# Fetching the last unit's other pair early, and splitting the last transfers over two queues, in an attention and MLP block

## The chip, the cores and the metric

The kernel runs on one core of a Trainium2 chip. The metric is the time of one execution in device microseconds (us), less being better. The core has a matrix engine (TensorE, "PE" in the profile, its weight loads "PEld"), a vector engine (VectorE, "DVE"), an activation engine (ScalarE, "ACT"), GpSimd ("POOL"), and SyncE ("SP"), which here does nothing but issue transfers. A row with "ACTq" or "SPq" is a transfer being issued from ACT or from SP.

## The reference

One input of 2048 tokens by 640 features is normalised. One branch is self-attention with 32 heads of 20 features, the other a two-layer MLP with 1536 hidden features and a normalisation of its own; the output is input plus both branches, in float32.

```python
def _A_ref(x, wqkv, wo):
    qkv = (x @ wqkv).reshape(B, S, 3, H, Dh).transpose(2, 0, 3, 1, 4)
    q, k, v = qkv[0], qkv[1], qkv[2]
    scores = jnp.einsum("bhqd,bhkd->bhqk", q, k) * (Dh ** -0.5)
    p = _softmax(scores, axis=-1)
    o = jnp.einsum("bhqk,bhkd->bhqd", p, v)
    return o.transpose(0, 2, 1, 3).reshape(B, S, D) @ wo

def _B_ref(x, w1, b1, w2, b2):
    y = _layernorm(x, axis=-1)
    h = _gelu(jnp.einsum("bsd,df->bsf", y, w1) + b1)
    return jnp.einsum("bsf,fd->bsd", h, w2) + b2

xn = _layernorm(x, axis=-1)
return x + _A_ref(xn, A_wqkv, A_wo) + _B_ref(xn, B_w1, B_b1, B_w2, B_b2)
```

## The kernel before

**Attention.** The heads are taken in 16 pairs, and the 2048 queries in two halves of 1024 (`hf` 0 and 1). For a pair and a half, `scores` (L680, exponential on ACT in L682) makes blocks of 128 keys by 512 queries for both heads, and `pv` (L711) multiplies them with the values. Values carry a column of ones, so the product `o` holds the unnormalised results and the softmax sums together. It has two parts `p` for either head, which are to be added. After 512 queries ACT reads `o` out into `ev` (L732); after 1024, `unload` writes the sums to the DRAM tensor `lpart` and the results to `opart`.

**Units and finishing.** Pairs are finished in units of three or two (`UNITS`). `finish` loads a unit's two parts of the sums into `lt` and of the results into `oa`, adds the parts of the sums, takes the reciprocal (L810 to L817), spreads it over the rows, adds the parts of the results (L835), multiplies (L837), splits the product into two float16 halves (L839, L841) and stores them in `oscr` (L842). `ready[hf]` counts the finished units of a half.

**The last unit** is pairs 14 and 15 of half 1. Its last pair never goes through DRAM: its rows of `lt` and `oa` are copied from `ev` itself (L778, L805), those of pair 14 come from `lpart` and `opart` (L774, L802). All these transfers are issued from ACT, because `dma` chooses ACT's queue for the last pair. For this unit the reciprocals are spread by sixteen products on PE with a selection matrix `sel` into a PSUM tile `rb` (L826), one of the three buffers of the pool `psS`.

**Projection.** `projection` multiplies `oscr` with the output weights in eight chunks of 256 tokens. A chunk has four groups of 15 products `z` (L1024). After each group DVE adds the result to the rows of `acc` (L983), and after two groups SP issues the store of the output (L987). Chunks 0 to 3 need half 0 alone, chunks 4 to 7 need the last unit too. `load_piece` has SP issue two transfers for `ot` (L977) and one for `acc` (L978). Behind the loop over the blocks (`ended`), the groups of `z` take their PSUM tiles from `psS`, the pool that `rb` is taken from.

**Order.** Every engine's order is written by hand. The loop calls `tick` after every two blocks of scores; `tick` advances all generators in `sides` by one step, so a `yield` in `finish` is a wait of one tick in the order, not a wait on the chip. Behind the loop one tick goes with three `z` products. `W1` is the number of ticks between the last unit's loads and the use of its sums, `W2` that between the spread reciprocals and the sum of the results.

**Completion semaphores.** The transfers issued from SP and ACT use eight completion semaphores in turn, counted in program order over both queues. A transfer therefore waits, on the engine that issues it, until the transfer eight places earlier has landed.

Of the kernel before, what the change touches and what calls it, by code (L numbers as in the profile page):

```python
# [7 lines left out]
F32 = mybir.dt.float32  # L8
# [8 lines left out]
P = 128  # L17
S, D, H, DH, F = 2048, 640, 32, 20, 1536
# [7 lines left out]
NPAIR = H // 2  # L26
# [7 lines left out]
UNITS = (3, 3, 3, 3, 2, 2)  # L34
# [8 lines left out]
def mha_mlp_kernel(tc, x, wqkv, wo, w1, b1, w2, b2, out):  # L43
    nc = tc.nc
# [3 lines left out]
    with (  # L48
# [13 lines left out]
        opart = dram.tile([2, D, S], F32, name="opart")  # L62
        lpart = dram.tile([2, 2, H, S // 2], F32, name="lpart")
# [529 lines left out]
        with ExitStack() as scope:  # L593
            pool = lambda **kw: scope.enter_context(tc.tile_pool(reuse_waits="tile", **kw))
            m0 = pool(name="m0", bufs=2)
            m1 = pool(name="m1", bufs=1)
            ptp = pool(name="pt", bufs=2 * GRP - 1)
# [3 lines left out]
            sides, patient = [], []  # L601
# [134 lines left out]
            def dma(g, hf):  # L736

                return (nc.scalar if (g, hf) == ORDER[-1] else nc.sync).dma_start
# [17 lines left out]
            fins, direct = [], []  # L756
            ready = [0, 0]

            def finishing():
                while fins:  # L760
                    yield from fins[0]
                    fins.pop(0)

            def finish(g0, g1, hf):
                nh, r0, r1 = 2 * (g1 - g0), 2 * g0 * DH, 2 * g1 * DH
                last = (g1 - 1, hf) == ORDER[-1]
                go = dma(g1 - 1, hf)
                w = 1024 if last else 512
                lt = m1.tile([P, 2, 64], F32, tag="lt", name="lt")
                n = checks.pop()  # L770
                yield
                gd = g1 - 1 if last else g1
                for p in range(2):
                    go(lt[: (gd - g0) * 32, p, :], lpart[p, hf, 2 * g0 : 2 * gd, :].rearrange("h (b t) -> (h b) t", t=64))  # L774
                    for a in range(2 if last else 0):

                        r = 64 * a + PAD + DH + VW * p
                        go(lt[(nh - 2 + a) * 16 : (nh - 1 + a) * 16, p, :],  # L778
                           direct[0][r : r + 1].rearrange("o c (b t) -> o (c b) t", t=64))
                for c0 in range(0, 1024, w):  # L780
                    cols = slice(hf * 1024 + c0, hf * 1024 + c0 + w)
                    if last:
                        o0, o1 = (ptp.tile([P, 2, 512], F32, tag="p", name="oa").rearrange("p c t -> p (c t)")
                                  for _ in range(2))
                        rb = o0

                        sel = [ptp.tile([P, 2, 512], F32, tag="p", name="sel").rearrange("p c t -> p (c t)")
                               for _ in range(2)]
                        for b0, t in zip((0, 8), sel):
                            nc.gpsimd.tensor_copy(  # L790
                                t[: nh * 16, : 8 * nh * DH].rearrange("p (b h d) -> p b h d", b=8, h=nh),
                                ident[: nh * 16, : nh * 16].rearrange("p (h b) -> p b h", b=16)[:, b0 : b0 + 8, :, None]
                                .to_broadcast([nh * 16, 8, nh, DH]))
                    else:
                        o = m1.tile([P, 2, 512], F32, tag="oa", name="oa")
                        o0, o1 = o[:, 0], o[:, 1]
                        rb = m1.tile([P, 512], F32, tag="rb", name="rb")
                    hl = o1.bitcast(F16).rearrange("p (s t) -> p s t", s=2)[: r1 - r0]
                    o0, o1, rb = o0[: r1 - r0], o1[: r1 - r0], rb[: r1 - r0]
                    rd = 2 * gd * DH - r0  # L800
                    for p, o in enumerate((o0, o1)):
                        go(o[:rd], opart[p, r0 : r0 + rd, cols])  # L802
                        for a in range(2 if last else 0):
                            q0 = 64 * a + PAD + VW * p
                            go(o[rd + a * DH : rd + (a + 1) * DH], direct[0][q0 : q0 + DH].rearrange("d c t -> d (c t)"))  # L805
                    if c0 == 0:
                        for _ in range(W1 if last else 4):
                            yield
                        l = lt[: nh * 16]
                        nc.vector.tensor_add(l[:, 0], l[:, 0], l[:, 1])  # L810

                        nc.vector.tensor_scalar(l[:, 1], l[:, 0], LO, None, ALU.is_ge, ALU.min,
                                                accum_out=good[: nh * 16, n : n + 1])
                        if not last:
                            yield
                        nc.vector.tensor_scalar(l[:, 0], l[:, 0], 1e-30, None, ALU.max)
                        nc.vector.reciprocal(l[:, 1], l[:, 0])  # L817
                        if not last:
                            go(linv[hf, 2 * g0 : 2 * g1, :].rearrange("h (b t) -> (h b) t", t=64), l[:, 1])
                        for _ in range(4 if last else 1):  # L820
                            yield
                    if last:

                        rb = psS.tile([P, 2, 512], F32, tag="s", name="rb")[: nh * DH]
                        for b in range(16):
                            nc.tensor.matmul(rb[:, b // 8, b % 8 * 64 : b % 8 * 64 + 64],  # L826
                                             sel[b // 8][: nh * 16, b % 8 * nh * DH : (b % 8 + 1) * nh * DH],
                                             l[:, 1], start=True, stop=True)
                        rb = rb.rearrange("p c t -> p (c t)")
                    for h in range(0 if last else nh):  # L830
                        go(rb[h * DH : (h + 1) * DH],
                           linv[hf, 2 * g0 + h : 2 * g0 + h + 1, c0 : c0 + w].to_broadcast([DH, w]))
                    for _ in range(W2 if last else 4):
                        yield
                    nc.vector.tensor_add(o0, o0, o1)  # L835
                    yield
                    nc.vector.tensor_mul(o0, o0, rb)  # L837
                    yield
                    nc.vector.tensor_copy(hl[:, 0], o0)  # L839
                    yield  # L840
                    nc.vector.tensor_sub(hl[:, 1], o0, hl[:, 0])  # L841
                    go(oscr[:, r0:r1, cols].rearrange("s d t -> d s t"), hl)  # L842
                ready[hf] += 1
# [111 lines left out]
            def mlp():  # L955
                load_chunk(0)
                load_chunk(1)
                yield 0.0
                for mc in range(NMC + 1):
                    first = [layer1(mc, f) for f in range(0, KF, 2)] if mc < NMC else []  # L960
                    second = [layer2(mc - 1, j, hf) for j in range(MC // P) for hf in range(2)] if mc else []
                    done[0] = mc == NMC
                    for i in range(6):
                        for part in first[i : i + 1] + (second[i - 1 : i] if i else []):
                            yield from part
# [29 lines left out]

            done = [False]
            ended = [False]
            W1, W2 = 12, 9

            def projection():  # L1000
                known = lambda c: split_done and ready[2 * c // NMC] == len(UNITS)
# [48 lines left out]
            def chain():  # L1050
                yield from mlp()
                yield from projection()


            with tc.manual_schedule():
                fill = chain()
                credit = 0.0 - next(fill)
                rate = 1.235
                groups = [(g, hf, cc, kb) for g, hf in ORDER for cc in range(2) for kb in range(0, NKB, GRP)]
# [40 lines left out]
                        sides.append(load_stack(*n, *([stacks[g, hf][1]] if n[0] == g else [])))  # L1100
                n = 0
                ended[0] = True

                def more(k):
                    nonlocal n
                    for _ in range(k):
                        n += 1
                        cost = next(fill, 0)
                        if n % 1 == 0 or cost is None:
                            tick()  # L1110
                        if cost == 0:
                            return False
                    return True
# [107 lines left out]
```

## Time and profile before

| | |
|---|---|
| three runs | 1362.19, 1363.1 and 1364.39 us; median 1363.1 us |
| the profiled execution | 1364.71 us |
| its span, first to last instruction | 1363.0 us |
| granted clock of TensorE over the span | 0.998 |
| PE busy | 1335.1 us, 98% |
| ACT busy | 1129.6 us, 83% |
| DVE busy | 1060.5 us, 78% |
| last read-out of `o` (L732) | 1290.43 us |
| last product starts its DVE step (L983) | 1356.27 us |

Times within the profile are counted from the start of the span. A row of the timeline gives start, length, engine, line, operation and tiles; rows of one kind that follow each other are merged, with their number. In brackets stands the idle time before it and what ended that. The length of an issue row (ACTq, SPq) is the time that the engine's queue takes to issue, not the transfer's time.

### The profile page before, as it was taken

How to read it: one execution, taken by the hardware profiler on the slowest of the kernel's cores; microseconds unless marked ns; L12 is line 12 of the kernel's file. 1: busy time of each engine (PE TensorE's matmuls, PEld its weight loads, DVE VectorE, ACT ScalarE, POOL GpSimd, SP SyncE). 2: the span in 40 equal slices, each digit the busy share in tenths (PEclk: the TensorE clock that was granted, in tenths of full speed). 3: DMA queues.
4: the chain of work that ended last, by engine and by line, in shares of the span. 5: the costliest groups of instructions: out<-in, count | busy, mean ns of one | idle time of the engine just before them, and what ended most of it. 6: DMA issues, size and time to landing. Idle time of an engine off the chain costs nothing.

```text
span 1363.0 us, 29029 instructions
## 1 busy us (share of the span) xinstructions
PE 1335.1 (98%) x11651; PEld 591.6 (43%) x11651; DVE 1060.5 (78%) x1436; ACT 1129.6 (83%) x1305; POOL 30.2 (2%) x74
## 2 busy tenths in 40 slices
PE   9999999999999999999999999999999999999998
PEld 6545545443334334433433343434433333333465
DVE  6658835998779897978797789897879898888732
ACT  6654525999999999999999999999999999999700
POOL 2000000000000000000000000000000000000000
PEclk9999999999999999999999999999999999999999
DMA  9868731111113221212321141223032223244275
GB/s 269 270 157 154 146 101 57 34 52 43 48 58 94 62 83 60 52 50 84 93 71 51 37 109 48 86 62 86 19 87 85 70 81 86 59 135 118 88 233 175
DMA packets 103073, 127.94 MB, mean 94 GB/s; under 512 B 27516, under 2 KB 69568, under 8 KB 102932
## 3 DMA queue, kind: packets, MB, share of 16 engines
q1 hardware_dynamic: 99864, 119.60, 31.2%
q0 software_dynamic: 2304, 5.24, 2.4%
q8 instruction: 93, 1.52, 0.5%
q10 hardware_dynamic: 764, 1.18, 0.3%
q14 instruction: 48, 0.39, 0.1%
HBM read 80.50 MB, written 42.51 MB: 90 GB/s over the span
## 4 chain that ended last, share of the span: by engine, by line
PE 79%; DVE 9%; ACT 7%; issue 3%; DMA 2%; ACTq 0%; SPq 0%; DVEq 0%
PE o L711 26%; PE s L680 17%; PE py L945 11%; PE pu L913 9%; PE qkp L322 8%; PE vp L395 5%; ACT p L682 4%; PE z L1024 4%; DVE low L694 3%; DMA oa<-ev 1%; DVE u L849 1%; DMA qkscr<-qkhl 1%; DVE u L850 1%; DVE w L853 1%; DVE w L854 1%
## 5 line engine op out<-in xcount | busy, mean ns | idle before, releaser
L682 ACT ACTIVATE p<-s 128x1024 f32<-128x1024 f32 x1024 | 972.3, 1041 | 43.4 <-PE s L680 37.0
L694 DVE TENSOR_TENSOR low<-p 128x1024 f16<-128x1024 f32 x512 | 610.7, 1219 | 159.9 <-ACT p L682 159.7
L711 PE MATMUL o<-p,vfull 128*32 128x512 bf16 (+1 forms) x4096 | 430.8, 493 | 0.0
L680 PE MATMUL s<-qs,ks 61*128 61x512 f16 x2048 | 316.5, 382 | 7.4 <-ACT p L682 6.5
L680 PEld LDWEIGHTS <-ks 61*128 61x128 f16 x2048 | 63.7, 94 | 293.6 <-issue 291.3
L913 PE MATMUL pu<-xm,w1t 128*128 128x256 f16 x1440 | 179.3, 274 | 1.4 <-DVE u L849 1.4
L945 PE MATMUL py<-w2t,hT 128*128 128x320 f16 x1152 | 178.5, 300 | 1.5 <-DVE u L849 1.5
L913 PEld LDWEIGHTS <-w1t 128*128 128x128 f16 x1440 | 130.5, 98 | 68.8 <-issue 55.1
L945 PEld LDWEIGHTS <-hT 128*128 128x128 f16 x1152 | 102.4, 98 | 88.6 <-issue 54.3
L322 PE MATMUL qkp<-xnt,wv 128*128 128x512 f16 x600 | 132.7, 383 | 2.3 <-DVE qkhl L338 2.1
L711 PEld LDWEIGHTS <-vfull 128*32 128x32 f16 x3072 | 60.8, 95 | 139.8 <-issue 108.5
L711 PE MATMUL o<-low,vfull 128*32 128x512 f16 x1024 | 104.0, 378 | 4.3 <-DVE low L694 4.3
L322 PEld LDWEIGHTS <-wv 128*128 128x128 f16 x600 | 58.7, 99 | 73.2 <-issue 2.6
L711 PEld LDWEIGHTS o<-p,vfull 128*32 128x32 f32 x2048 | 62.6, 108 | 51.3
L337 ACT ACTIVATE qkhl<-qkp,qks 128x1024 f16<-128x1024 f32 (+1 forms) x24 | 23.2, 968 | 66.5 <-PE qkp L322 43.3
L1024 PE MATMUL z<-w1t,ot 128*128 128x320 f16 x480 | 66.7, 300 | 1.8 <-DVE oa L837 1.8
L395 PE MATMUL vp<-wv,xnt 128*128 128x320 f16 x480 | 66.7, 299 | 0.0
L338 DVE SCALAR_TENSOR_TENSOR qkhl<-qkp,qks,qkhl 128x1024 f16<-128x1024 f32 (+1 forms) x24 | 26.5, 1105 | 45.3 <-ACT qkhl L337 44.5
L1024 PEld LDWEIGHTS <-ot 128*128 128x128 f16 x480 | 46.3, 98 | 23.1 <-issue 2.9
L395 PEld LDWEIGHTS <-xnt 128*128 128x128 f16 x480 | 46.7, 98 | 18.7
L983 DVE SCALAR_TENSOR_TENSOR acc<-z,sc,acc 128x320 f32<-128x320 f32 x32 | 17.5, 550 | 43.2 <-PE z L1024 39.9
L732 ACT ACTIVATE ev<-o 128x512 f32<-128x512 f32 x64 | 39.2, 612 | 4.2 <-PE o L711 4.1
(179 smaller groups left out, 666.7 us busy)
## 6 DMA issues: line engine op xcount, KB each, us to landing
qkscr<-qkhl SPq DMA_DIRECT2D x40, 256.0 KB
opart<-ev SPq DMA_DIRECT2D x124, 80.0 KB
ks<-qkscr SPq DMA_DIRECT2D x120, 80.0 KB
qs<-qkscr SPq DMA_DIRECT2D x192, 40.0 KB
oa<-opart SPq DMA_DIRECT2D x32, 240.0 KB
xt<-in_A_x_dram SPq DMA_DIRECT2D x16, 320.0 KB
xscr<-xnt SPq DMA_DIRECT2D x4, 1280.0 KB
xm<-xscr SPq DMA_DIRECT2D x8, 640.0 KB
```

Source lines behind the costliest of these rows:

```text
L322: nc.tensor.matmul(ps[:, i, :], wv[:, k, q, a, mm * P : (mm + 1) * P], xnts[c][:, k, b, :], start=(k + n == 0), stop=(k == KD - 1 and n == 2))
L337: nc.scalar.activation(hl[:, 0, i0:i1], ps[:, i0:i1], AF.Copy, scale=a)
L338: nc.vector.scalar_tensor_tensor(hl[:, 1, i0:i1], ps[:, i0:i1], a, hl[:, 0, i0:i1], ALU.mult, ALU.subtract)
L395: nc.tensor.matmul(ps[:, hf, :320], xnts[c][:, k, a, j * P : (j + 1) * P], wv[:, k, 2, b, hf * 320 : (hf + 1) * 320], start=(n == 0), stop ...
L680: nc.tensor.matmul(ps[:, a, :], ks[64 * a : 64 * a + 61, kb * P : (kb + 1) * P], qs[64 * a : 64 * a + 61, cc * 512 : (cc + 1) * 512], star ...
L682: nc.scalar.activation(pt, ps, AF.Exp, scale=QS)
L694: nc.vector.tensor_sub(low, pt, upper(pt))
L711: nc.tensor.matmul(pv.o[32 * q : 32 * q + 32, :], src[:, v0 - PAD * (1 - q % 2) :][:, :32], t, start=q not in pv.begun, stop=last, skip_gr ...
L732: nc.scalar.activation(evs[g, hf][:, cc], pv.o, AF.Copy)
L913: nc.tensor.matmul(ps[:, i], w1v[:, k, (f + i) // 4, a, fo_ : fo_ + P], xnt[:, k, b, :], start=(n == 0), stop=(n == 3 * KD - 1))
L945: nc.tensor.matmul(ps[:, :320], hTs[mc][:, f, a, j * P : (j + 1) * P], w2v[:, f, b, hf * 320 : (hf + 1) * 320], start=(n == 0), stop=(n == ...
L1024: nc.tensor.matmul(ps[:, :320], ot[:, k, a, j * P : (j + 1) * P], wov[:, k, b, h * 320 : (h + 1) * 320], start=(n == 0), stop=(n == 3 * KD ...
```

## The change

A generator `fetch_sums` runs with the other side work and, once five units of half 1 are finished, has SP issue the two loads of pair 14's sums into `lt`. A function `fetch_results` is called at the loop's end and has SP issue the two loads of pair 14's results into the two `oa` tiles. The last unit's `finish` takes these tiles and no longer issues those four loads. Its four copies of sums from `ev` stay on ACT's queue; its four copies of results from `ev` go to SP's queue. `W1` becomes 10 instead of 12, `W2` 5 instead of 9.

The order of instructions that results: PE's spread products `rb` stand six `z` products earlier (48 of them stand between the end of the last `pv` and `rb`, against 54). On DVE the four steps on the sums stand one L983 earlier, L835 and L837 one L983 earlier, and L839 and L841 two and one. On SP the two loads of sums stand ahead of a store to `accscr`, the two loads of results ahead of a store of the output, and the four copies of results between that store and the next. Nothing else is moved on PE, DVE or ACT. The two copies of `sel` on POOL take buffers that come free later, the first behind one and the second behind the next group of value products.

```diff
+            fetched = []
+
+            def fetch_sums():
+                while ready[1] < len(UNITS) - 1:
+                    yield
+                lt = m1.tile([P, 2, 64], F32, tag="lt", name="lt")
+                r = 2 * (NPAIR - UNITS[-1])
+                for p in range(2):
+                    nc.sync.dma_start(lt[: 32 * (UNITS[-1] - 1), p, :],
+                                      lpart[p, 1, r : 2 * NPAIR - 2, :].rearrange("h (b t) -> (h b) t", t=64))
+                fetched.append(lt)
+
+            def fetch_results():
+                r0, r1 = 2 * (NPAIR - UNITS[-1]) * DH, (2 * NPAIR - 2) * DH
+                for p in range(2):
+                    o = ptp.tile([P, 2, 512], F32, tag="p", name="oa").rearrange("p c t -> p (c t)")
+                    nc.sync.dma_start(o[: r1 - r0], opart[p, r0:r1, 1024:])
+                    fetched.append(o)
...
-                lt = m1.tile([P, 2, 64], F32, tag="lt", name="lt")
+                lt = fetched.pop(0) if last else m1.tile([P, 2, 64], F32, tag="lt", name="lt")
...
-                    go(lt[: (gd - g0) * 32, p, :], lpart[p, hf, 2 * g0 : 2 * gd, :].rearrange("h (b t) -> (h b) t", t=64))
+                    if not last:
+                        go(lt[: nh * 16, p, :], lpart[p, hf, 2 * g0 : 2 * g1, :].rearrange("h (b t) -> (h b) t", t=64))
...
-                        o0, o1 = (ptp.tile([P, 2, 512], F32, tag="p", name="oa").rearrange("p c t -> p (c t)")
-                                  for _ in range(2))
+                        o0, o1 = fetched
...
-                        go(o[:rd], opart[p, r0 : r0 + rd, cols])
+                        if not last:
+                            go(o[:rd], opart[p, r0 : r0 + rd, cols])
                         for a in range(2 if last else 0):
                             q0 = 64 * a + PAD + VW * p
-                            go(o[rd + a * DH : rd + (a + 1) * DH], direct[0][q0 : q0 + DH].rearrange("d c t -> d (c t)"))
+                            nc.sync.dma_start(o[rd + a * DH : rd + (a + 1) * DH],
+                                              direct[0][q0 : q0 + DH].rearrange("d c t -> d (c t)"))
...
-            W1, W2 = 12, 9
+            W1, W2 = 10, 5
...
                 fill = chain()
+                sides.append(fetch_sums())
...
                 ended[0] = True
+                fetch_results()
```

## The prediction

> **What bounds the kernel now.** I read the page first, for the engine that is full: the busy shares and the shares of the chain that ended last.
>
> ```profile
> span 1363.0 us, 29029 instructions
> PE 1335.1 (98%) x11651; PEld 591.6 (43%) x11651; DVE 1060.5 (78%) x1436; ACT 1129.6 (83%) x1305; POOL 30.2 (2%) x74
> PE 79%; DVE 9%; ACT 7%; issue 3%; DMA 2%; ACTq 0%; SPq 0%; DVEq 0%
> ```
>
> PE is busy for 98% of the span and carries most of the chain. The change neither removes a product nor adds one, so it can win only time in which PE stands still. The edit acts behind the last value products; I read the chain of waits from there on, in order of time (start, length, what).
>
> ```profile
> 1290.43 0.61 ACT ev L732
> ...
> 1291.06 0.64 ACTq L778
> ...
> 1294.98 5.30 DMA oa<-ev
> ...
> 1300.31 5.90 DMA oa<-ev
> ...
> 1306.40 1.23 DVE oa L835
> ...
> 1307.65 1.23 DVE oa L837
> ...
> 1308.93 40.67 PE z L1024 x297
> 1349.60 0.11 PE pb L1047
> ...
> 1356.27 0.55 DVE acc L983
> ```
>
> For 18 us the chain is off PE: the read-out, issues on ACT one behind the other, a copy of results that lands 5.3 us after its issue began, another that could be issued only then (it reuses the first one's completion semaphore) and takes 5.9, then two DVE steps; then PE goes on. What PE itself lost stands in the timeline.
>
> ```profile
> 1290.29 7.51 PE L1024 MATMUL z<-w1t,ot 128*128 128x320 f16 x54
> 1298.04 2.47 PE L826 MATMUL rb<-lt,sel 64*80 64x64 f32 x32 [0.24 <-issue]
> 1300.44 6.69 PE L1024 MATMUL z<-w1t,ot 128*128 128x320 f16 x48
> 1308.93 40.67 PE L1024 MATMUL z<-w1t,ot 128*128 128x320 f16 x297 [1.79 <-DVE oa L837]
> 1315.46 33.80 PEld L1024 LDWEIGHTS <-ot 128*128 128x128 f16 x250 [0.31 <-DMA ot<-oscr]
> 1323.56 0.55 DVE L983 SCALAR_TENSOR_TENSOR acc<-z,sc,acc 128x320 f32<-128x320 f32 x1 [1.49 <-PE z L1024]
> 1325.59 0.55 DVE L983 SCALAR_TENSOR_TENSOR acc<-z,sc,acc 128x320 f32<-128x320 f32 x1 [1.49 <-PE z L1024]
> ```
>
> Ends on PE are modelled, so I count from starts. The last two rows are one undisturbed group of 15 products apart; from 1323.56 to the last L983 at 1356.27 are 16 groups and the 0.11 of `pb`, so 2.04 us a group, 0.136 a product. The 54 products from 1290.29 should end at 1297.62, and `rb` starts at 1298.04: 0.42 lost. The 48 from 1300.44 should end at 1306.96, and the next starts at 1308.93: 1.97 lost, the wait for L837, which reads `rb` and so holds one of the three `psS` buffers. The 345 from 1308.93 on should take 46.9 with `pb`, to 1355.8; with the run of the last product (54 take 7.51 instead of 7.33, so 0.17) to 1356.0, and the last L983 starts at 1356.27: 0.2 lost, the wait for `ot`. Together 2.6 us: all that PE loses behind the last read-out, and the ceiling of the gain.
>
> **The change part by part.** *The sums.* Six issues for them before, and the DVE steps that use them:
>
> ```profile
> 1291.06 1.27 ACTq L778 DMA_DIRECT2D lt<-ev  x2
> 1292.37 0.59 ACTq L774 DMA_DIRECT2D lt<-lpart  x1
> 1293.00 1.15 ACTq L778 DMA_DIRECT2D lt<-ev  x2
> 1294.17 0.55 DVE L983 SCALAR_TENSOR_TENSOR acc<-z,sc,acc 128x320 f32<-128x320 f32 x1 [1.48 <-PE z L1024]
> 1296.68 0.21 DVE L810 TENSOR_TENSOR lt<-lt 64x64 f32<-64x64 f32 x1
> 1297.39 0.55 DVE L817 RECIPROCAL lt<-lt 64x64 f32<-64x64 f32 x1
> 1294.50:1295.00 0.50, 0.50 (x6) 0.37 (x4) 0.22 (x1) 0.00 (x0) 0.00 (x0) 1.00 0.05 8
> 1240.25 0.47 SPq L819 DMA_DIRECT2D linv<-lt  x1
> 1242.02 1.40 SPq L831 DMA_DIRECT2D rb<-linv  x4
> ```
>
> The last copy of sums began its issue at about 1293.55 and was used at 1296.68, so it landed in 3.1 us at most. The nearest short transfer, `linv`, could be read again 1.8 us after its issue began. With `lpart` out of the queue the four copies go at 0.64 each from 1291.06, the last at about 1293.0; landing 1294.8 to 1296.1. The DVE steps now stand behind the L983 that ends at 1294.72 and take 1.26 (1296.68 to 1297.94): done between 1296.1 and 1297.4. PE arrives at `rb` after 48 products, at 1296.8. I take the lower end, since the DMA engines were nearly empty in that window (share 0.05, the last figure but one), and a start of `rb` at about 1296.9. After `rb` nine products of the group are left instead of three. Before, 54 products and `rb` were through at 1300.44; now at 1296.9 + 2.4 + 6 × 0.136 = 1300.1. Gain 0.3; by the upper end 0.3 is lost.
>
> *The results.* The copies before, what SP issued at the same time, and issues of the same row size from SP:
>
> ```profile
> 1294.98 1.63 ACTq L805 DMA_DIRECT2D oa<-ev  x2
> 1295.19 1.07 SPq L977 DMA_DIRECT2D ot<-oscr  x2
> 1309.82 1.05 SPq L977 DMA_DIRECT2D ot<-oscr  x2
> 1262.41 0.80 SPq L748 DMA_DIRECT2D opart<-ev  x2
> 1288.92 6.18 SPq L987 DMA_DIRECT2D out_dram<-acc  x2
> ```
>
> An issue costs 0.4 (`opart`, SP) to 0.8 (ACT). Two queues issuing at once do not slow each other: the pair of `ot` takes 1.07 beside ACT's copies and 1.05 alone. So four copies start on SP from 1291.06 to at most 1293.5. None waits long for a semaphore: the fourth reuses that of the store issued at 1288.92. With the durations 5.3 and 5.9, both taken beside the loads of `ot` and `acc`, they land at 1299.4 at the latest. The sum of the results stands on DVE behind the L983 of the group in which `rb` lies: nine products after `rb` end at 1300.5, that L983 at about 1301.2. So the transfers are covered by 1.8 us; the two steps of 1.23 end at 1303.7. Of the three buffers, that of `rb` is wanted by the third group from there, which PE reaches at 1300.5 + 2 × 2.04 = 1304.6. PE no longer waits: gain 1.97. If the cover goes, PE waits from a landing after 1302.0 on.
>
> *A rule on queues.* On queues, the Trainium skill, "DMA: Bandwidth & Descriptors", section "Issuing engines are not separate DMA queues", speaks against this part: transfers from several engines share the same 16 DMA engines, and a second issuing engine saves only issue time, usually small beside the transfer. By that rule the second queue alone brings little. Here the engines were at 0.05 while ACT issued, and ten issues and a semaphore stood between read-out and the last copy, so I count on issue time, and weigh the rule as the second rival.
>
> *What is moved ahead.* The two loads of sums go to SP between a store of `oscr` and one of `accscr`, the two of results to the gap ahead of the store at 1288.92:
>
> ```profile
> 1272.97 0.34 SPq L842 DMA_DIRECT2D oscr<-oa  x1
> 1275.71 0.34 SPq L883 DMA_DIRECT2D accscr<-xb  x1
> 1277.26 0.56 SPq L978 DMA_DIRECT2D acc<-accscr  x1
> 1286.80 0.90 POOL L790 COPY sel<-ident 64x640 f32<-64x640 f32 x1 [33.69 <-PE o L711]
> 1311.22 0.38 ACTq L842 DMA_DIRECT2D oscr<-oa  x1
> ```
>
> SP is idle for 2.4 us in the first gap and 11.1 in the second, so both are free; the loads of results wait there for value products before the last group, and behind them stands only the store at 1288.92, which nobody waits for until `acc` is loaded again. The selections on POOL wait for later value products, but those end before 1290.43, and the copies take 0.9 or less each; PE wants them at 1296.8.
>
> *Queued behind the copies on SP* are a store, then `ot` and `acc` of the third chunk. The first `ot` reuses the semaphore of the first copy, so it starts at 1297.0 at the latest instead of 1295.19. PE needs it at 1304.6. The pair issued at 1309.82 was there at 1315.46, 5.6 later; by that it is there at 1302.6. No cost. The `ot` of the fourth chunk, at which PE lost 0.2, is issued behind a store that waits for two L983; these now end at about 1306.7, so it goes at 1307.1, 2.7 earlier than 1309.82, while PE wants it 2.3 to 2.4 earlier. The store of `oscr`, issued at 1311.22 behind it, now runs just ahead of it. I take 0.1 of the 0.2; the bounds are 0.2 gained and, if `oscr` costs it one more us, 0.8 lost.
>
> *Sum.* 0.3 + 1.97 + 0.1 = 2.4 us, bounds 0.9 (−0.3, 1.97, −0.8) and 2.6. The profiled execution took 1364.71 (1.7 outside its span); 1362.3 is expected for it. The median of the runs is 1.6 below it, and by the same sum 1363.1 becomes 1360.7.
>
> **Rivals.** *Half the gain.* The wait for `ot` of the fourth chunk grows as just said, or the sums land at the upper end. For: the row at 1315.46 shows that this load was already late. Against: it moves as far as PE does. Around 1.2 is won: 1361.9.
>
> *The results land as late as before* (the rule's case: the transfers, not their issue, are the limit). This is the rival on the other side. In the new order `rb`'s buffer is wanted one group earlier than before, since L837's place in the order is earlier: 87 `z` products precede that point, 102 did. Landed at 1306.2 as before, PE would go on at 1308.8 with one group more to do: 2.0 less 0.2 at the `ot` wait, 1364.9. It decides from a landing of 1304.5 on, where the wait at that place equals all that was lost before. For: both copies on record took over 5 us for 80 KB. Against: they ran beside `ot` and `acc`, and now begin 4 to 7 us before these.
>
> *The sums land late.* With four copies of results in flight they could take what those took, 5.9 us: landed at 1298.9, `rb` at 1300.3, 3.0 lost against 2.0 won elsewhere: 1364.1. It turns at a landing of 1298.0, 5.0 after issue. Against it speaks the 3.1 us bound.
>
> **How the numbers follow.** About 0.2%, 2.7 us, is what a measurement can tell from no change here: the three runs span 2.2. The forecast has 0.74, half the gain 0.10, the late results 0.09, the late sums 0.07. The forecast's 2.4 lies just short of 2.7, and a median of such runs moves by about one us; half of its chance, 0.37, falls beyond, with 0.03 of the second case: faster 0.40. Slower beyond 2.7 needs half of the late results and a third of the late sums: 0.07. The rest, 0.53, is within. The forecast's own range is 1359.6 to 1361.9; to leave out no more than two in ten the range goes on through half the gain towards the others: 1359.5 to 1363.3.
>
> **What would show it.** Right: four issues of L799 and four of L827 side by side on ACT and SP from 1291.06; the sums added at about 1295; no idle PE over 0.3 us between 1290 and 1308; the store of `oscr` 5 us earlier than 1311.22; the last L983 near 1353.9. Wrong: idle PE ahead of `rb`, DVE waiting for a copy into `oa`, or PE waiting for L860; and any change before 1290.29 beyond a tenth or two.

## The result, and the profile after

| | before | after |
|---|---|---|
| median of 12 runs each | 1362.78 us | 1360.53 us |
| the profiled execution | 1364.71 us | 1360.14 us |
| its span | 1363.0 us | 1358.4 us |
| last read-out (L732) to last DVE step on `z` (L983, after: L1006) | 65.84 us | 63.47 us |

The three runs of before known ahead are among its 12. The ratio of after to before is 0.9984, 95% interval 0.9976 to 0.9992: 2.2 us less, within 0.2%, with an interval that does not reach 1. A second set of runs gave 0.9985, 0.9976 to 0.9994.

The profiled execution is 4.6 us shorter, twice as much as the medians say. Line L732 shows which part to leave out (the answer on one line: times, engine, count, shortest/median/longest in ns, start of the first and the last). The first row is before, the second after, the third e2, a kernel of the experiments below with other transfers at the end:

```profile
L732 ACT ACTIVATE ev<-o x64: 597/599/647, 242.8 to 1290.4; 128x512 f32<-128x512 f32 x64
```
```profile
L732 ACT ACTIVATE ev<-o x64: 596/600/649, 240.4 to 1288.1; 128x512 f32<-128x512 f32 x64
```
```profile
L732 ACT ACTIVATE ev<-o x64: 597/600/650, 244.3 to 1291.9; 128x512 f32<-128x512 f32 x64
```

From first to last read-out all three take 1047.6 or 1047.7 us. They differ ahead of 245 us, where the three kernels have the same instructions. A part of this is TensorE's granted clock: its mean over the first 50 us was 0.97 in both traces of before, 1.00 in both of after and 0.95 in e2. The rest stays open, since e6, e7 and e8 had 1.00 there and a late read-out too. So single executions are compared here by the stretch behind the last read-out, in which the 2.37 us lie. Two executions of before gave 65.84 and 65.71, two of after 63.47 and 63.49.

Page and chain of waits of after, as shown for before:

```profile
span 1358.4 us, 29032 instructions
PE 1333.2 (98%) x11651; PEld 591.3 (44%) x11651; DVE 1060.7 (78%) x1436; ACT 1129.7 (83%) x1305; POOL 30.1 (2%) x74
PE 79%; DVE 9%; ACT 7%; issue 3%; DMA 2%; SPq 0%; ACTq 0%; DVEq 0%
```
```profile
1286.34 1.65 PE o L711 x16
1287.99 6.62 PE z L1047 x48
1294.61 2.46 PE rb L849 x32
1297.07 47.79 PE z L1047 x351
1344.86 0.11 PE pb L1070
1344.97 6.53 PE z L1047 x48
1351.53 0.55 DVE acc L1006
```

The chain no longer leaves PE: read-out, issues, transfers and both DVE steps have gone from it. On the page all this is invisible, since 2.4 us in 1360 move a share by rounding at most. The timeline shows what became of the old chain (a selection of its rows):

```profile
1287.92 6.69 PE L1047 MATMUL z<-w1t,ot 128*128 128x320 f16 x48
1288.06 0.60 ACT L732 ACTIVATE ev<-o 128x512 f32<-128x512 f32 x1 [2.47 <-PE o L711]
1288.68 3.15 SPq L827 DMA_DIRECT2D oa<-ev  x4
1288.69 2.64 ACTq L799 DMA_DIRECT2D lt<-ev  x4
1291.80 0.55 DVE L1006 SCALAR_TENSOR_TENSOR acc<-z,sc,acc 128x320 f32<-128x320 f32 x1 [1.48 <-PE z L1047]
1292.86 1.06 SPq L1000 DMA_DIRECT2D ot<-oscr  x2
1293.22 0.22 DVE L833 TENSOR_TENSOR lt<-lt 64x64 f32<-64x64 f32 x1 [0.87 <-DMA lt<-ev]
1293.95 0.55 DVE L840 RECIPROCAL lt<-lt 64x64 f32<-64x64 f32 x1
1294.60 2.47 PE L849 MATMUL rb<-lt,sel 64*80 64x64 f32 x32
1297.00 47.86 PE L1047 MATMUL z<-w1t,ot 128*128 128x320 f16 x351
1298.91 1.21 DVE L858 TENSOR_TENSOR oa<-oa 80x1024 f32<-80x1024 f32 x1
1300.15 1.22 DVE L860 TENSOR_TENSOR oa<-oa,rb 80x1024 f32<-80x1024 f32 x1
1303.71 0.40 ACTq L865 DMA_DIRECT2D oscr<-oa  x1
```

Sums and results are issued side by side. L858 stands right behind the DVE step before it and waits for no transfer, where L835 had waited for the second copy. Against the beat of 0.136 us a product, `rb` starts 0.16 behind the 48 products, and nothing is lost between `rb` and the end beyond about 0.1. Only L833 waits now, 0.87 for the last sums; nearly all of that is hidden, as e8 shows, where this wait is gone and `rb` still starts 0.1 behind the products.

### The profile page after: what moved, and what is told of

The parts are those of the page before. It is cut to its first block, busy times and chain, and to the rows that moved or that the text cites. A ratio compares the mean times of both kernels' runs of the same rounds, so it can differ in the third digit from the quotient of the medians.

```text
span 1358.4 us, 29032 instructions
## 1 busy us (share of the span) xinstructions
PE 1333.2 (98%) x11651; PEld 591.3 (44%) x11651; DVE 1060.7 (78%) x1436; ACT 1129.7 (83%) x1305; POOL 30.1 (2%) x74
## 4 chain that ended last, share of the span: by engine, by line
PE 79%; DVE 9%; ACT 7%; issue 3%; DMA 2%; SPq 0%; ACTq 0%; DVEq 0%
PE o L711 26%; PE s L680 16%; PE py L968 11%; PE pu L936 9%; PE qkp L322 7%; PE z L1047 5%; ACT p L682 4%; PE vp L395 4%; DVE low L694 3%; DMA qkscr<-qkhl 1%; DVE u L872 1%; DVE u L873 1%; DVE w L876 1%; DVE w L877 1%; ACT wv L428 1%
## 5 line engine op out<-in xcount | busy, mean ns | idle before, releaser
L1006 DVE SCALAR_TENSOR_TENSOR acc<-z,sc,acc 128x320 f32<-128x320 f32 x32 | 17.3, 546 | 42.9 <-PE z L1047 36.8
L732 ACT ACTIVATE ev<-o 128x512 f32<-128x512 f32 x64 | 39.1, 612 | 4.2 <-PE o L711 4.1
```

The source lines that it names most:

```text
L732: nc.scalar.activation(evs[g, hf][:, cc], pv.o, AF.Copy)
```

## Experiments

The change has three parts: the early loads, the second queue, the shorter ticks. Theory A: PE's wait for the buffer of `rb` is a matter of when the copies of results land against where the order wants that buffer; any part that makes them land in time removes it. Theory B: the parts are all needed. The first six kernels, with before and after, are all eight combinations of the three parts.

**e1: early loads and second queue, old ticks.**

```diff
-            W1, W2 = 10, 5
+            W1, W2 = 12, 9
```

> The changed kernel with W1, W2 back at 12 and 9. The measure beside the time is the stretch from the start of the last read-out (L732) to the start of the last DVE step on z: 65.84 us before, 63.47 after. Theory A, what wins is that the results land before DVE wants them, and the ticks only place the steps: rb starts after 54 products without a wait, the sum of the results stands behind one more step on DVE and ends about 1.3 us before its buffer is wanted: stretch 63.3 to 63.6, time 2.2 us under before. Theory B, the ticks are part of the gain: PE waits for the buffer of rb again: stretch 64.5 to 65.8.

Measured: ratio 0.9988 (0.9980 to 0.9997), stretch 63.71. As A expects, but for 0.1 of stretch: by the beat `rb` starts 0.4 late, as before the change, since L833 stands behind a third L1006 again. The time, 1.6 us under before, leaves A's 2.2 within its interval. The ticks are worth 0.24 us here, which no time can show.

**e3: second queue alone.**

```diff
-                        go(o[:rd], opart[p, r0 : r0 + rd, cols])
+                        nc.sync.dma_start(o[:rd], opart[p, r0 : r0 + rd, cols])
...
-                            go(o[rd + a * DH : rd + (a + 1) * DH], direct[0][q0 : q0 + DH].rearrange("d c t -> d (c t)"))
+                            nc.sync.dma_start(o[rd + a * DH : rd + (a + 1) * DH], direct[0][q0 : q0 + DH].rearrange("d c t -> d (c t)"))
```

> The kernel before with all six transfers of results on the queue of SP; nothing is fetched early, W1 and W2 stay at 12 and 9. Theory A, either half of the change removes the wait of 1.97 us: six sums on ACT and six results on SP side by side, the last copy of results issued about 4.6 us after the read-out and landed before the sum of the results wants it; the wait ahead of rb (0.4) stays: stretch 63.8 to 64.1, time 1.8 to 2.0 us under before. Theory B, the early loads are what matters, since twelve transfers share eight completion semaphores on two queues as on one: stretch 65 to 66.

Measured: 0.9983 (0.9974 to 0.9992), stretch 63.72, just under what A expects; the time, 2.3 us under before, is above its 2.0, with an interval that holds it. The whole wait for L837 is gone. The order fetches nothing early, but on SP the first load from `opart` (L802) no longer stands behind the sums: it is issued 1.05 us ahead of the read-out, where before it was issued 3.8 behind it.

**e6: early loads alone.** The changed kernel with the copies of results back on ACT and the old ticks.

```diff
-                            nc.sync.dma_start(o[rd + a * DH : rd + (a + 1) * DH],
+                            go(o[rd + a * DH : rd + (a + 1) * DH],
...
-            W1, W2 = 10, 5
+            W1, W2 = 12, 9
```

> The early loads alone: the changed kernel with the copies of results behind those of sums on the queue of ACT and W1, W2 at 12 and 9. With the shorter ticks the same transfers landed 12.9 us after the read-out began and PE waited 1.1 us. Theory A, the transfers end the wait only up to the place that the order gives the buffer of rb: with the old ticks that buffer is wanted one group later, 16.5 us after the read-out, and the copies, landed by 13, are in time: stretch 63.7 to 64.2, time 1.6 to 2.2 us under before. Theory B, one queue is too slow whatever the order: stretch 65 to 66.

Measured: 0.9990 (0.9981 to 0.9999), stretch 63.72. The time, 1.4 us under before, is below A's 1.6, with an interval that holds it. The early loads alone remove the wait too. They are issued from SP, so this part also takes four issues off ACT's queue; whether the earlier start or the shorter queue is what counts in it was not tested. So either of the two big parts does what both do together (e1, 63.71).

**e4: shorter ticks alone.**

```diff
-            W1, W2 = 12, 9
+            W1, W2 = 10, 5
```

> The kernel before with W1, W2 at 10 and 5 and no transfer moved. The mechanism of the second rival of the prediction: the results land as late as before, about 15.8 us after the read-out starts, and the buffer of rb is wanted one group of z earlier: PE waits there for about 4 us instead of 2: stretch 67.3 to 67.9, time 1.5 to 2.0 us over before. The other view, DVE and PE reorder around the wait and the place in the order means nothing: stretch 65.8, time as before.

Measured: 1.0033 (1.0020 to 1.0046), stretch 68.10. The waits of that stretch (who <- for whom: us in total, times, longest):

```profile
DVE oa L835 <- DMA oa<-ev: 4.9, 1, 4.9
PE z L1024 <- DVE oa L837: 4.0, 1, 4.0
```

This is the second rival of the prediction on the chip: the results land as late as before, the buffer is wanted a group earlier, and PE waits 4.0 us where it had waited 1.8. The time was 4.5 us over before, twice what this stretch shows, so it was run once more:

> The ticks alone once more: the kernel before with W1, W2 at 10 and 5. Its first run gave a stretch of 68.10 us in the profile (2.3 over before) but a time 4.5 us over. If the wait varies from run to run, the stretch comes out otherwise here, between 67 and 70, and the time again 2 to 5 us over; if the first time was a scatter of few runs, the time is 2.0 to 2.6 us over before.

Measured: 1.0029 (1.0020 to 1.0039), 4.0 us; stretch 69.27. The wait for L837 is 4.0 again, and then:

```profile
1307.71 10.53 PE L1024 MATMUL z<-w1t,ot 128*128 128x320 f16 x64 [4.00 <-DVE oa L837]
```

64 products should take 8.7 and took 10.5, so PE lost some 1.7 more inside this row, where in the first execution 62 products took 8.58 with no loss. It is not a wait for a transfer. The DVE steps (L983) of the first two groups behind the wait show where it lies: they start at 1310.93 and 1313.66, 2.73 apart, and then one follows every 2.04 again. In those groups the granted clock was low. A row of this view gives a stretch, its length, the busy time of PE, PEld, DVE, ACT and POOL, then the granted clock and two figures on DMA; the first row is this execution, the second the same place in the first one:

```profile
1308.70:1312.10 3.40, 3.40 (x15) 1.96 (x14) 2.19 (x4) 0.00 (x0) 0.00 (x0) 0.51 0.40 99
```
```profile
1308.30:1311.70 3.40, 3.40 (x28) 2.45 (x26) 2.21 (x5) 0.00 (x0) 0.00 (x0) 1.00 0.39 97
```

3.4 us at 0.51 of the clock are 1.7 lost. Behind the same wait of 4.0 us the clock stayed at 1.00 in one execution and fell in the other. This fits a time that exceeds the stretch: of the 17 runs of e4, the nine with a mean granted clock of 0.996 or less took 1367.84 to 1370.81 us, the other eight 1365.55 to 1368.79. Two of the 63 runs of before beside them had so low a clock. Where in the runs without a trace the clock fell is not shown.

**e2: early loads and shorter ticks, one queue.** The first hunk of e6 without the second.

> The changed kernel with the four copies of results on the queue of ACT, behind the four of sums; the early loads and the ticks stay. Theory A, issue order and early loads carry it, and the second queue only saves some 2.6 us of issuing: the last copy is issued 5.0 us after the first copy of sums instead of 2.4 after, lands 5 to 6 us later, and DVE waits for it by at most 0.7 us, which the buffer rotation hides: stretch 63.5 to 63.9, time 1.9 to 2.3 us under before. Theory B, the second queue is needed: DVE waits over 2 us for the copies, PE behind it: stretch over 65.

Measured: 0.9992 (0.9982 to 1.0002), stretch 65.35. This went against A, and the stretch is in B's range: the copies landed later than I allowed, and with the shorter ticks the queue did matter. In time order:

```profile
1295.19 3.64 ACTq L827 DMA_DIRECT2D oa<-ev  x4
1296.69 1.51 SPq L1000 DMA_DIRECT2D ot<-oscr  x2
1298.72 0.37 SPq L1001 DMA_DIRECT2D acc<-accscr  x1
1304.80 1.22 DVE L858 TENSOR_TENSOR oa<-oa 80x1024 f32<-80x1024 f32 x1 [1.99 <-DMA oa<-ev]
1307.42 8.58 PE L1047 MATMUL z<-w1t,ot 128*128 128x320 f16 x62 [1.12 <-DVE oa L860]
```
```profile
1298.10 6.68 DMA oa<-ev
```

The last copy, issued at 1298.10 (the chain's row, below), took 6.7 us, with `ot` and `acc` beside it; DVE had it 12.9 us after the read-out. By the beat PE lost 1.3 us there, and some 0.6 more further on, most of it at the `ot` of the fourth chunk, which is issued 2.1 us later than in after. In e6 the same transfers were in time because the old order wants the buffer later. The Trainium skill ("DMA: Bandwidth & Descriptors", section "Issuing engines are not separate DMA queues") says that a second issuing engine saves issue time alone, usually small beside the transfer. e6 agrees with its main point, since without the second queue for the copies nothing is lost there. In e2 the 2.6 us of issue time were not small: they put the last copy among the loads.

**e5: second queue and shorter ticks, no early loads.** e3 with W1, W2 at 10 and 5.

> The kernel before with its six transfers of results on the queue of SP and W1, W2 at 10 and 5: the change without any early load. Stretch from the last read-out to the last DVE step on z: 65.84 us before, 63.47 after the change, 63.72 with the queue alone. Theory A, the second queue carries the gain and the early loads add nothing on their own: the last of six sums is issued 3.2 us after the read-out begins, lands 1.8 to 2.5 us later, rb starts up to 0.6 us later than with the change: stretch 63.4 to 64.0, time 1.8 to 2.4 us under before. Theory B, the early loads are needed for the shorter ticks: the copies of results land later than 11 us after the read-out, PE waits for the buffer of rb: stretch over 65.

Measured: 0.9989 (0.9979 to 0.9998), stretch 64.16, a little above what A expects; the time gain of 1.5 us is below its 1.8, with an interval that holds both.

```profile
1293.36 0.22 DVE L810 TENSOR_TENSOR lt<-lt 64x64 f32<-64x64 f32 x1 [1.57 <-DMA lt<-ev]
1294.73 2.47 PE L826 MATMUL rb<-lt,sel 64*80 64x64 f32 x32 [0.68 <-issue]
```

With six sums on ACT DVE waits 1.57 for them and PE stands idle 0.68 us ahead of `rb`; by the beat `rb` comes 0.85 late, against 0.16 in after. This is the one place where the early loads pay once the second queue is there: 0.7 of stretch, and only because the shorter ticks want the sums earlier.

The eight combinations, stretch in us (two executions where two stand):

| | old ticks | shorter ticks |
|---|---|---|
| neither | 65.84, 65.71 (before) | 68.10, 69.27 (e4) |
| early loads | 63.72 (e6) | 65.35 (e2) |
| second queue | 63.72 (e3) | 64.16 (e5) |
| both | 63.71 (e1) | 63.47, 63.49 (after) |

**e7: do the copies take over 5 us by themselves?** Before, with the loads of the third chunk two groups later.

```diff
-                            if j + h > 0 and c + 1 < NMC and c + 1 not in pieces and known(c + 1):
+                            if j + h > (c == 1) and c + 1 < NMC and c + 1 not in pieces and known(c + 1):
```

> The kernel before, with the loads of ot and acc for the third chunk moved two z groups later, behind the next store of the output; nothing else. Theory A, the copies of results from ACT take 5.3 and 5.9 us only because they run beside these loads: they land in about 3.5 us each, the last about 11 to 12 us after the read-out instead of 15.8, DVE no longer waits for them and PE not for the buffer of rb: stretch 63.8 to 64.8 (the upper end if ot itself now comes up to a us late), time 1 to 2 us under before. Theory B, a copy of 20 rows of 4 KB takes over 5 us by itself: the last lands at 15 us or later, stretch 65.5 or more.

Measured: 1.0014 (1.0004 to 1.0023), stretch 67.92. A holds for the copies and fails for the time.

```profile
1294.83 1.63 ACTq L805 DMA_DIRECT2D oa<-ev  x2
1297.06 1.53 ACTq L805 DMA_DIRECT2D oa<-ev  x2
1301.91 1.04 SPq L977 DMA_DIRECT2D ot<-oscr  x2
1303.42 1.21 DVE L835 TENSOR_TENSOR oa<-oa 80x1024 f32<-80x1024 f32 x1
1306.98 0.57 PE L1024 MATMUL z<-w1t,ot 128*128 128x320 f16 x2 [2.03 <-DVE oa L839]
1308.01 10.24 PE L1024 MATMUL z<-w1t,ot 128*128 128x320 f16 x65 [0.46 <-DMA ot<-oscr]
```

By the semaphore events of the traces (a transfer has landed with the last event of its semaphore) the four copies took 3.50, 3.09, 3.08 and 2.64 us, where before they took 5.30, 5.46, 7.32 and 5.90. The second pair is issued in 1.53 us, where before it took 3.84. The reason is a second effect of this edit: with three transfers fewer ahead of it, the last copy takes the semaphore of the last sums, landed at 1295.12, and no longer that of the first copy. L835 waits for no transfer.

But `ot` is now late by some 2.5 us at the third chunk: its two loads landed at 1306.93 and 1307.97. (The wait that ended at 1306.98 is put down to L839, which ended at that time too; but the weight loads of the same products wait for `ot` in the view.) Another 1.2 is lost within the last row, 65 products in 10.24, since the granted clock was low behind this wait:

```profile
1307.20:1310.90 3.70, 3.24 (x15) 1.69 (x14) 1.00 (x1) 0.00 (x0) 0.00 (x0) 0.54 0.88 288
```

I had allowed one us for all of this. So the collision of the copies with the loads of `ot` and `acc` is what made them slow, and two groups later is too late for these loads.

**e8: both queues take sums first.** The one wait left in after is L833's. Here part 0 goes to ACT and part 1 to SP, sums ahead of results.

```diff
-                        go(lt[(nh - 2 + a) * 16 : (nh - 1 + a) * 16, p, :],
+                        (go, nc.sync.dma_start)[p](lt[(nh - 2 + a) * 16 : (nh - 1 + a) * 16, p, :],
...
-                            nc.sync.dma_start(o[rd + a * DH : rd + (a + 1) * DH],
+                            (go, nc.sync.dma_start)[p](o[rd + a * DH : rd + (a + 1) * DH],
```

> The changed kernel with the copies from the last read-out split over the queues by part instead of by kind: the sums of part 0 and then its results on ACT, those of part 1 on SP. Theory A, in the changed kernel the sums are late by 0.9 us on DVE because four of them go one behind the other beside the copies of results; two and two first, they are there when DVE comes: rb starts 0.1 to 0.2 us earlier, stretch 63.2 to 63.4, time 2.2 to 2.5 us under before, no difference from the change that times can tell. Rival, issuing is not the limit of the sums: DVE still waits for them 0.5 us or more, stretch 63.5.

Measured: 0.9978 (0.9969 to 0.9987), stretch 63.44. DVE no longer waits for the sums:

```profile
1290.24 6.69 PE L1047 MATMUL z<-w1t,ot 128*128 128x320 f16 x48
1294.12 0.55 DVE L1006 SCALAR_TENSOR_TENSOR acc<-z,sc,acc 128x320 f32<-128x320 f32 x1 [1.49 <-PE z L1047]
1294.59 0.21 DVE L833 TENSOR_TENSOR lt<-lt 64x64 f32<-64x64 f32 x1
1296.87 2.50 PE L849 MATMUL rb<-lt,sel 64*80 64x64 f32 x32
```

The wait was nearly hidden already, so `rb` gains hardly anything (0.1 lost instead of 0.16) and the stretch is that of after to 0.03. The time is 3.0 us under before, more than A's 2.2 to 2.5, with an interval that holds these. That this version beats after is not shown, since the intervals of 0.9978 and 0.9984 overlap for the most part.

**after_again, before_again.** Both kernels unaltered.

> The changed kernel unaltered, once more beside before. If the gain lies in the stretch behind the last read-out alone, the stretch is again 63.3 to 63.7 while the start of the read-out moves by up to 2 or 3 us between executions; time 2.2 to 2.5 us under before, if the gain is from elsewhere the stretch or the ratio moves.

> The kernel before unaltered, one more look at its stretch: 65.4 to 66.4 if the landing of the copies beside the loads of ot and acc is steady, with a read-out that starts up to 2 or 3 us earlier or later than 1290.43.

Measured: after 0.9985 (0.9976 to 0.9994), stretch 63.49, read-out at 1288.54; before one execution of 1364.93 us, stretch 65.71, read-out at 1290.57. For these two kernels the stretch repeats within 0.15 us; the read-out moves between 1287.5 and 1291.9 over all executions.

## Why the prediction was right, point by point

- **The ceiling.** PE's lost time counted by the beat was the right measure. Of 2.6 us predicted as the most, 2.37 came; what is left is 0.16 ahead of `rb` and about 0.1 further on. The forecast of 1353.9 for the last L983 holds when it is counted from the read-out: 1290.43 + 63.47.
- **The sums, 0.3.** Measured 0.26 (0.42 lost before, 0.16 after). The sum held with a term that was mis-sized: I took the landing near its lower end, 1.8 to 2.0 us after the issue. The last copy's issue began at 1290.62 and it landed at 1293.05, 2.4 us later. The DVE steps ended at 1294.5, when PE came. It was right with no margin, by luck of 0.1. I had reasoned that the DMA engines were nearly empty in that window; in the new order the copies of results are in it, and they cost the sums up to 0.7 (last section).
- **The results, 1.97.** Measured whole. Four issues took 3.15, the upper end of 0.4 to 0.8 each. The transfers took 2.4 to 2.6 each, not the 5.3 and 5.9 taken as bounds, so the last one landed at 1293.50, 4.9 us ahead of the L1006 in front of L858, where 1.8 had been forecast. That two queues do not slow each other rested on one pair of issues: the pair of `ot` took 1.06 in after, as forecast, but 1.51 beside ACT's copies in e2 and e6.
- **The `ot` of the fourth chunk, 0.1.** About 0.1; in after it was issued 16.5 us after the read-out instead of 19.4, as PE's need moved.
- **Early loads on SP at no cost.** Held: with the old ticks and the second queue, the early loads change the stretch by 0.01 at most (e1 against e3).
- **The second rival** did not occur in after, but e4 shows that its mechanism is real. Its price was put at 1.8 us and came out at 2.3 and 3.5 in the stretch, 4.0 to 4.5 in time. The wait for `rb`'s buffer was sized nearly right (4.0 instead of 1.8, so 2.2); left out were the `ot` of the fourth chunk, at which PE waited 0.3 in one execution, and the granted clock, which cost 1.7 in the other.
- **The late sums** did not occur; 2.4 us is half the 5.0 at which that rival turns.
- **One sign I named was not met**: the time before the read-out changed by 2.4 us. It lies in the first 245 us and does not follow the change: e1, e2, e6 and e8 have the early loads and read out at 1290.2 to 1291.9, later than after's 1288.06; e3 and e5 have none and read out at 1287.5 to 1288.0.
- **What the prediction did not see** is that the parts overlap. I added them up as one step; either big part alone removes the 1.97, and the ticks, which I had costed only through `rb`, are worth 0.24 with both and cost 0.4 to 3.5 without.

## What to carry to other kernels

Count an engine's lost time from the starts of its instructions and the beat of an undisturbed stretch; here that gave the ceiling, and the ceiling was nearly the result. A wait of this kind has two ends, when the transfer lands and where the order wants the buffer that depends on it: moving the second without the first (e4) made the kernel 4 us slower, moving the first in either of two ways was enough as long as the second stayed (with the shorter ticks the early loads alone were not, e2). Look at the granted clock of a slow row before putting it down to a wait: in e4 and e7 up to 1.7 us looked like one. Where two parts each look like the whole gain, run them apart before adding them up.

## What the runs showed of the hardware that was not expected

A copy's time depended on what was issued around it more than on its size. By the semaphore events the four 80 KB copies took 2.4 to 2.6 us each in after, where all are issued ahead of the loads of `ot`; 2.6 to 3.5 in e7, where these loads are moved away; 5.3 to 7.3 before, beside `ot` and `acc`; and 2.6, 4.6, 5.6 and 6.7 in e2, where the loads begin between them.

The four 4 KB copies of sums took 1.69 to 1.74 us each in e2, where the copies of results stand behind them on the same queue, and 1.69, 2.18, 2.24 and 2.43 in after, where these run beside them. The two kernels differ in nothing else, so the copies of results are what slowed the sums.

The granted clock fell to about half behind some waits of PE and not behind others: to 0.51 over 3.4 us behind a wait of 4.0 us in the second execution of e4, and to 0.54 over 3.7 us behind one of 2.0 in e7; the first execution of e4 kept 1.00 behind 4.0, and before kept it behind 1.8. What decides it is not shown.
